# Cosine attention and a leaky-relu MLP in one kernel: a written instruction list up to the third batch's second unit, and float32 sums of the last three groups' exponentials on VectorE

## The chip, the cores and the metric

The kernel runs on one core of one Trainium2 chip. The metric is the device time of one execution in microseconds (us); three runs of the kernel before gave 415.45, 415.52 and 416.83, median 415.52.

## The reference

Inputs are q, k and v (8 batches, 12 heads, 448 positions, 64 per head), a scalar tau, and two weight matrices. What is computed, cut to what matters:

```python
q_n = q / (norm(q, axis=-1) + 1e-6);  k_n = k / (norm(k, axis=-1) + 1e-6)
scores = q_n @ k_n.T / tau            # tau = 0.1, per head
attn = exp(scores - max) / (sum(exp(scores - max)) + 1e-9)
x = (attn @ v) reshaped to (3584 tokens, 768)
h = x @ w_in                          # 768 x 2048
out = maximum(0.01 * h, h) @ w_out    # 2048 x 768, float32
```

## The kernel before

**Stages of attention.** Heads go in pairs; a slot is what is normalised at a time. Each slot's rows are loaded by a DMA that SP issues (`load_qk`, L141 to L163), squared on POOL (L218, L226; three slots at the start on ACT), summed on VectorE (L234, L240), turned into norms on ACT (`roots`, two small activations, L247 and L248) and scaled on VectorE (`normalise`, L255 to L272). For the first two batches TensorE transposes the result (L286) and VectorE copies it back (L327). From the third batch on, VectorE transposes it (L308) and six small DMAs of SP per unit spread it (L317). A unit is two pairs of heads; it has seven key tiles.

**Scores.** The score matmuls take 64 rows of the array (L348 for the first two batches, L419 after that) and write pairs of PSUM banks; ACT takes the exponential of 128x896 elements at a time into a bfloat16 tile `pe` (L357, L425). **Sums and products.** The row totals are matmuls with a weight of ones: for the first two batches `totals` (L368), then `group_products(g, None)` (L444): 7 key tiles x 4 strips x 2 halves, 56 matmuls of 64x32 weights and 448 columns. A logarithm and an exponential on ACT invert them (L379/L380, L453/L456). The products with v are 48 or 56 matmuls more per half of the head (L368, L444), and VectorE scales them into `xT` (L399, L469, L475). A group is one or two units (`GROUPS`): groups 7, 8 and 9, the last three, are units 12 to 17.

**The MLP.** Tokens go in eight chunks, 384 or 512 columns in turn. `first(c, m)` (L496) multiplies 6 slices of `w_in` with `xT` for each of 16 rows of blocks m; ACT applies the leaky relu into `hT` (L507), of which there is one buffer, so a chunk's relus wait for the chunk before to be read. `second(c, ts, half)` (L533) is 16 matmuls of 384 columns; VectorE copies the result (L543) and SP writes it out (L550).

**What sets the order.** Every engine runs its instructions in the order in which the program states them. The head of the program (the first two batches) is written as calls in loops and lists. From the third batch on, loops walk through *visits* of three key tiles; a planner with weights and due times feeds `first` and `second` groups between them. `fill` (L607) is a matmul on a constant tile that keeps TensorE running at the start; `WARM = 20` of them stand ahead of the first transposes. `hold` (L618) is a tiny POOL copy that makes POOL wait for a normalised slot before its next squares or DMA; `hold_loads` (L615) does the same on SP's queue. The eight PSUM banks are dealt by age, at the start with pairs and singles in separate halves.

Of the kernel before, what the change touches and what calls it, by code (L numbers as in the profile page):

```python
# [12 lines left out]
AX = mybir.AxisListType  # L13


@with_exitstack
def kernel(
# [25 lines left out]
    WARM = 20  # L43
    NEWQ = 2 * NQ
    PER = 3
# [5 lines left out]
    vbp = ctx.enter_context(tc.tile_pool(name="vb", bufs=3))  # L51
# [19 lines left out]
    age = [0] * 8  # L71
    kept = {}
    deals = {"n": 0, "apart": True, "width": 128}

    def banks(count, keep=None):
        lo, hi = (0, 8) if not deals["apart"] else (0, 4) if count == 2 else (4, 8)
        x = min(
            (i for i in range(lo, hi, count) if not set(range(i, i + count)) & set(kept.values())),
            key=lambda i: max(age[i : i + count]),
        )  # L80
        deals["n"] += 1
        age[x : x + count] = [deals["n"]] * count
        if keep:
            kept[keep] = x
        return ps[:, x] if count == 1 else ps[:, x : x + count]

    def given_back(keep):
        deals["n"] += 1
        age[kept.pop(keep)] = deals["n"]

# [21 lines left out]
    raw = {}  # L117
# [55 lines left out]
    def load_v(j):  # L173
        if j >= B * NQ:
            return
        b, jj = divmod(j, NQ)
        vb[j] = vbp.tile([128, 4, 3, D], BF16, name="v_b")
        gp.dma_start(out=vb[j], in_=main(v, b, 4 * jj, 4))
# [32 lines left out]
    def squares(s, eng=gp, parts=(0, 1)):  # L211
        if s >= NSLOT:
            return
        sq = sqt[s % 3]
        if s >= OLD:
            sqs[s] = sq
            x = raw[s].rearrange("p (t d) -> p t d", d=D)
            gp.tensor_tensor(sq[:, :, :D], x, x, op=ALU.mult)  # L218
            return
        sqs[s] = halves(sq.rearrange("p t d -> p (t d)"), D + 1)  # L220
        for i in parts:
            x, y = raw[s][i], sqs[s][i]
            if eng is nc.scalar:
                nc.scalar.activation(y[..., :D], x, func=AF.Square)
            else:
                eng.tensor_tensor(y[..., :D], x, x, op=ALU.mult)  # L226

    def sums(s, parts=(0, 1)):
        if s >= NSLOT:
            return  # L230
        if s not in ss:
            ss[s] = smp.tile([128, 14], F32, name="ss")
        if s >= OLD:
            nc.vector.tensor_reduce(  # L234
                ss[s], sqs[s], axis=AX.X, op=ALU.add
            )
            return
        for i in parts:
            o = ss[s][:, 0:8] if i == 0 else ss[s][:, 8:14]
            nc.vector.tensor_reduce(  # L240
                o.rearrange("p (h t) -> p h t", h=2), sqs[s][i], axis=AX.X, op=ALU.add
            )

    def roots(s):
        if s >= NSLOT:
            return
        nc.scalar.activation(ss[s], ss[s], func=AF.Ln)  # L247
        nc.scalar.activation(norms[s % 3][:, :, 0], ss[s], func=AF.Exp, scale=0.5)  # L248
# [3 lines left out]
    def normalise(s):  # L252
        if s >= NSLOT:
            return
# [29 lines left out]
    def one(tp, s, lo, hi):  # L284
# [10 lines left out]
    def transposed():  # L295
        return banks(1).bitcast(BF16)[:, : 7 * 128].rearrange("p (t c) -> p t c", c=128)
# [3 lines left out]
    def transposes(s):  # L300
        if s >= NSLOT:
            return
        if s >= OLD:
            u, which = divmod(s - OLD, 2)
            if which == 0:
                turned[u] = ttp.tile([128, 2, 2, S], BF16, name="tt")
            to = turned[u][:, :, which].bitcast(F32)
            nc.vector.transpose(  # L308
                out=to.rearrange(("p g (c m) -> p m g c", "p g (m c) -> p m g c")[which], m=7),
                in_=qn[s].bitcast(F32).rearrange("p m (g c) e -> p m g (c e)", g=2),  # L310
            )
            if which == 0:
                return
            for w, pair in enumerate(UNITS[u][1]):
                dst = qtp.tile([128, 2, S], BF16, name="qkT")
                for r0, of, n, g in ((0, 0, 32, 0), (32, 0, 64, 1), (96, 32, 32, 0)):
                    nc.sync.dma_start(  # L317
                        out=dst[r0 : r0 + n],
                        in_=turned[u][64 * w + of : 64 * w + of + n, g],
                    )  # L320
                qkT[pair] = dst.rearrange("p t c -> p (t c)")
            return
        dst = qtp.tile([128, 7, 128], BF16, name="qkT")
        qkT[s] = dst.rearrange("p t c -> p (t c)")
        tp = transposed()
        one(tp, s, 0, 7)
        nc.vector.tensor_copy(out=dst, in_=tp)  # L327
# [6 lines left out]
    def scores(s, kis):  # L334
        key_tiles([(s, ki) for ki in kis])

    def key_tiles(which):

        tiles = []
        for s, ki in which:  # L340
            sc = banks(2)
            tiles.append(sc)
            width = deals["width"] if ki < 3 else min(deals["width"], 64)
            for p in range(0, 128, width):
                x, c0 = (qkT[s - 1 + p // 64], 448 + p % 64) if ki == 3 else (qkT[s], 512 + 128 * ki + p)
                for a in range(2):
                    rows = slice(64 * a, 64 * a + 64)
                    nc.tensor.matmul(  # L348
                        out=sc[p : p + width, a, :S], lhsT=x[rows, c0 : c0 + width],
                        rhs=x[rows, 0:S], start=True, stop=True,  # L350
                    )
        for (s, ki), sc in zip(which, tiles):
            if ki == 3:
                dst = pr[s // 2] = pe_tile()
            else:
                dst = pe[s, ki] = pe_tile()
            nc.scalar.activation(out=dst, in_=sc[:, :, :S], func=AF.Exp, scale=inv_tau)  # L357
# [17 lines left out]
    def totals(j):  # L375
        sm = banks(1)
        strip_products(j, sm, lambda g, ki: ones, lambda g: ones_rem[:, g // 2])
        rb = rbp.tile([128, 2, S], F32, name="rb")[:, 0]
        nc.scalar.activation(rb, sm[:, :S], func=AF.Ln)  # L379
        nc.scalar.activation(rb, rb, func=AF.Exp, scale=-1.0)  # L380
        rbs[j] = rb

    pos = {}

    def products(j, e, po=None):
        b, jj = divmod(j, NQ)
        if po is None:
            po = banks(1, (j, e))
        pos[j, e] = po
        vm = vb[j].rearrange("p h t (d e) -> p h t e d", e=2)  # L390
        vr = vrb[b % 2].rearrange("p j g (d e) -> p j g e d", e=2)
        strip_products(j, po, lambda g, ki: vm[:, g, ki, e], lambda g: vr[:, jj, g, e])

    def scale(j, e):
        b, jj = divmod(j, NQ)
        m, half = divmod(b, 2)
        if m not in xT:
            xT[m] = xtp.tile([128, KT, 2 * S], BF16, name="xT")
        nc.vector.tensor_tensor(  # L399
            xT[m][:, 2 * jj + e, half * S : (half + 1) * S], pos.pop((j, e))[:, :S], rbs[j],  # L400
            op=ALU.mult,
        )
        if (j, e) in kept:
            given_back((j, e))
# [3 lines left out]
    def quad_tiles(which):  # L408

        tiles = []  # L410
        for u, i in which:
            sc = banks(2)
            tiles.append(sc)
            for strip in range(4):
                x = qkT[UNITS[u][1][strip // 2]]
                c0 = S + 64 * i + 32 * (strip % 2)
                for a in range(2):
                    rows = slice(64 * a, 64 * a + 64)
                    nc.tensor.matmul(  # L419
                        out=sc[32 * strip : 32 * strip + 32, a, :S], lhsT=x[rows, c0 : c0 + 32],  # L420
                        rhs=x[rows, 0:S], start=True, stop=True,
                    )
        for (u, i), sc in zip(which, tiles):
            pq[u, i] = pe_tile()
            nc.scalar.activation(out=pq[u, i], in_=sc[:, :, :S], func=AF.Exp, scale=inv_tau)  # L425
# [3 lines left out]
    def group_products(g, e):  # L429


        us = [u for u, (gg, _) in enumerate(UNITS) if gg == g]
        two = len(us) == 2
        po = banks(2)
# [14 lines left out]
        return po  # L449

    def group_logs(g, po):
        grb[g] = rbp.tile([128, 2, S], F32, name="rb")
        nc.scalar.activation(grb[g], po[:, :, :S], func=AF.Ln)  # L453
# [10 lines left out]
    def group_scale(g, e, po):  # L464
        js = GROUPS[g]
        for w in range(2):
# [6 lines left out]
            for n in range(2):  # L473
# [4 lines left out]
                )  # L478

# [7 lines left out]
    def first(c, m, kts=range(KT)):  # L487
        c0, n = chunk_cols(c)
        if c not in hT:
            hT[c] = htp.tile([128, MT, 512], BF16, name="hT")  # L490
        if (c, m) in begun:
            pm, done = begun.pop((c, m))
        else:
            pm, done = banks(1, (c, m, "begun") if len(kts) < KT else None), 0
# [7 lines left out]
        if done + len(kts) < KT:  # L502
            begun[c, m] = pm, done + len(kts)
            return
        if (c, m, "begun") in kept:
            given_back((c, m, "begun"))
# [491 lines left out]
```

## Time and profile before

| what | us |
|---|---|
| median of three runs | 415.52 |
| profiled execution, its own time | 416.8 |
| its span on the core | 415.0 |
| TensorE matmuls busy | 405.8 (98%) |
| ACT busy | 250.5 (60%) |
| VectorE busy | 221.4 (53%) |
| POOL busy | 115.1 (28%) |

The span runs from the first to the last instruction of the core; the execution's own time is 1.8 us longer. A line of the profile gives the source line, the engine, the operation with output and inputs, its count, the busy time and the mean duration of one. The chain of waits is the work that ended last, followed back; a row gives start, length and the line. TensorE's granted clock is 1.00 in all stretches.

### The profile page before, as it was taken

To read this page: it belongs to the slowest core of one execution; us is meant where nothing else is said; L and a number is where in the kernel's file an instruction comes from. 1 tells how busy PE (TensorE), PEld (TensorE's weight loads), DVE (VectorE), ACT (ScalarE), POOL (GpSimd) and SP (SyncE) were. 2 spreads that over 40 slices of the span, in tenths; PEclk is the share of its full clock that TensorE was granted. 3 is DMA by queue.
4 is the path that set the end of the run, shared out by engine and by line. 5 is a ranking of instruction groups with operands and counts; after the bars stand their busy time and mean duration, and the time that the engine had idled before them with its cause. 6 is when DMAs were issued, how large, how long until landed. Compare 5 with 4: busy or idle time off the path is not lost.

```text
span 415.0 us, 11326 instructions
## 1 busy us (share of the span) xinstructions
PE 405.8 (98%) x4783; PEld 212.2 (51%) x4799; DVE 221.4 (53%) x387; ACT 250.5 (60%) x431; POOL 115.1 (28%) x150
## 2 busy tenths in 40 slices
PE   8799999999999999999999999999999999999997
PEld 3235555544555555544455555554445555654465
DVE  5878879756778556766484964464621301210021
ACT  4997877378657785667865688547764464004300
POOL 4885556133234132413331433122210000000000
PEclk9999999999999999999999999999999999999999
DMA  7999998965377851884285681742442100020022
GB/s 184 233 208 222 216 232 176 258 178 127 57 208 184 206 127 24 206 230 97 51 190 153 149 235 44 173 128 84 91 90 66 53 39 3 38 77 0 2 76 76
DMA packets 41980, 53.82 MB, mean 130 GB/s; under 512 B 12490, under 2 KB 32330, under 8 KB 41930
## 3 DMA queue, kind: packets, MB, share of 16 engines
q1 hardware_dynamic: 25738, 41.01, 35.1%
q0 software_dynamic: 15504, 11.80, 19.8%
q8 instruction: 37, 0.61, 0.6%
q10 hardware_dynamic: 688, 0.30, 0.2%
q14 instruction: 13, 0.11, 0.1%
HBM read 45.61 MB, written 11.01 MB: 136 GB/s over the span
## 4 chain that ended last, share of the span: by engine, by line
PE 93%; DMA 2%; ACT 1%; POOL 1%; SPq 1%; issue 1%; DVE 0%; POOLq 0%
PE ps L533 36%; PE ps L496 36%; PE ps L444 9%; PE ps L419 7%; PE ps L368 3%; PE ps L348 2%; DMA xT<-in_k_dram 1%; DMA xT<-in_q_dram 1%; ACT pe L357 1%; POOL sq L226 1%; PE ps L286 1%; SPq L133 0%; DVE qn L272 0%; POOL v_rem L186 0%; SPq L141 0%
## 5 line engine op out<-in xcount | busy, mean ns | idle before, releaser
L533 PE MATMUL ps<-w_out_sb,hT 128*128 128x384 bf16 (+1 forms) x912 | 151.3, 323 | 0.0
L496 PE MATMUL ps<-xT,w_in_sb 128*128 128x384 bf16 (+1 forms) x754 | 150.1, 352 | 0.8 <-issue 0.2
L425 ACT ACTIVATE pe<-ps 128x896 bf16<-128x896 f32 x126 | 108.9, 916 | 47.1 <-PE ps L419 47.1
L533 PEld LDWEIGHTS <-hT 128*128 128x128 bf16 x912 | 86.5, 98 | 64.0 <-issue 10.3
L496 PEld LDWEIGHTS <-w_in_sb 128*128 128x128 bf16 x768 | 72.6, 98 | 74.3 <-issue 9.8
L507 ACT ACTIVATE hT<-ps 128x384 bf16<-128x384 f32 (+1 forms) x128 | 67.4, 553 | 56.1 <-PE ps L496 54.9
L543 DVE COPY osb<-ps 128x384 f32<-128x384 f32 (+1 forms) x57 | 31.2, 547 | 101.4 <-PE ps L533 101.3
L218 POOL TENSOR_TENSOR sq<-qk_h 128x896 f32<-128x896 f32 x36 | 60.9, 1691 | 13.0 <-DMA qk_h<-in_k_dram 8.5
L618 POOL CAST seen<-qn 128x1 f32<-128x1 bf16 x46 | 8.5, 185 | 166.3 <-DVE qn L262 156.5
L262 DVE TENSOR_TENSOR qn<-qk_h,r 128x896 bf16<-128x896 f32 x36 | 43.3, 1203 | 1.2
L234 DVE TENSOR_REDUCE ss<-sq 128x14 f32<-128x910 f32 x36 | 37.9, 1053 | 1.1 <-POOL sq L218 1.1
L357 ACT ACTIVATE pe<-ps 128x896 bf16<-128x896 f32 x42 | 36.0, 918 | 2.4 <-PE ps L348 2.3
L419 PE MATMUL ps<-qkT 64*32 64x448 bf16 x1008 | 36.5, 353 | 0.0
L255 DVE TENSOR_REDUCE r<-norms 128x14 f32<-128x28 f32 x48 | 8.6, 178 | 48.7 <-ACT norms L248 48.1
L469 DVE TENSOR_TENSOR xT<-ps,rb 128x448 bf16<-128x448 f32 x32 | 18.4, 615 | 23.2 <-PE ps L444 21.5
L308 DVE STREAM_TRANSPOSE tt<-qn 128x448 f32<-128x448 f32 x36 | 29.6, 821 | 0.9
L444 PE MATMUL ps<-pe,vq 64*32 64x448 bf16 x1008 | 27.0, 349 | 0.0
L247 ACT ACTIVATE ss<-ss 128x14 f32<-128x14 f32 x48 | 10.3, 215 | 23.6 <-DVE ss L234 23.1
L419 PEld LDWEIGHTS <-qkT 64*32 64x32 bf16 x1008 | 13.0, 91 | 19.2 <-issue 14.2
L444 PEld LDWEIGHTS <-vq 64*32 64x32 bf16 x1008 | 14.5, 92 | 8.0 <-issue 0.3
L444 PE MATMUL ps<-pe,ones 64*32 64x448 bf16 x560 | 15.1, 349 | 0.0
L348 PE MATMUL ps<-qkT 64*64 64x448 bf16 (+1 forms) x132 | 12.8, 359 | 2.1 <-ACT pe L357 1.2
(53 smaller groups left out, 218.1 us busy)
## 6 DMA issues: line engine op xcount, KB each, us to landing
qk_h<-in_q_dram SPq DMA_DIRECT2D x36, 224.0 KB, 4.1
qk_h<-in_k_dram SPq DMA_DIRECT2D x36, 224.0 KB, 4.6
out_dram<-osb SPq DMA_DIRECT2D x20, 384.0 KB, 2.3
qkT<-tt SPq DMA_DIRECT2D x72, 56.0 KB, 3.2
qkT<-tt SPq DMA_DIRECT2D x36, 112.0 KB, 3.4
vq<-in_v_dram POOLq DMA_DIRECT2D x16, 224.0 KB, 4.7
w_in_sb<-in_moe_w_in_dram POOLq DMA_DIRECT2D x4, 768.0 KB, 10.4
out_dram<-osb SPq DMA_DIRECT2D x15, 192.0 KB, 3.7
```

What stands on the lines that cost most here:

```text
L218: gp.tensor_tensor(sq[:, :, :D], x, x, op=ALU.mult)
L234: nc.vector.tensor_reduce(ss[s], sqs[s], axis=AX.X, op=ALU.add)
L262: nc.vector.tensor_tensor(qn[s].rearrange("p m d e -> p m e d"), raw[s].rearrange(f"p ({t[1:-1]} d) -> p m e d", e=n, d=D), r.rearrange(f" ...
L308: nc.vector.transpose(out=to.rearrange(("p g (c m) -> p m g c", "p g (m c) -> p m g c")[which], m=7), in_=qn[s].bitcast(F32).rearrange("p ...
L357: nc.scalar.activation(out=dst, in_=sc[:, :, :S], func=AF.Exp, scale=inv_tau)
L419: nc.tensor.matmul(out=sc[32 * strip : 32 * strip + 32, a, :S], lhsT=x[rows, c0 : c0 + 32], rhs=x[rows, 0:S], start=True, stop=True,)
L425: nc.scalar.activation(out=pq[u, i], in_=sc[:, :, :S], func=AF.Exp, scale=inv_tau)
L444: nc.tensor.matmul(out=po[32 * strip : 32 * strip + 32, w, :S], lhsT=weights, rhs=pq[us[x if two else 0], i][rows, a, :], start=(i == 0), ...
L496: nc.tensor.matmul(out=pm[:, :n], lhsT=w_in_sb[:, kt, m * 128 : (m + 1) * 128], rhs=xT[c // 2][:, kt, c0 : c0 + n], start=(done + i == 0), ...
L507: nc.scalar.activation(out=hT[c][:, m, :n], in_=pm[:, :n], func=AF.Prelu, alpha=0.01)
L533: nc.tensor.matmul(out=po2[:, : hi - lo], lhsT=hT[c][:, m, ts * 128 : (ts + 1) * 128], rhs=w_out_sb[:, m, half * HALF + lo : half * HALF + ...
L543: nc.vector.tensor_copy(out=o[:, cols], in_=po2[:, : hi - lo])
```

## The change

A string `ORDER` of 1,249 words now lists every step, and a loop calls them one after another; a word is a step's name with its numbers, as `f.0.5` for `first(0, 5)`. Steps that were one call are cut in two, so that the matmuls (`k`, `q`, `f`, `s`, `to`, `pr`, `g`) and what reads their banks (`x`, `y`, `r`, `o`, `ln`, `sc`, `gl`, `gx`) stand apart in the list. Three stretches can be told apart:

- **Up to `q.2.4`** (the fifth key tile of unit 2) the list is in a new order. 30 fills stand ahead of the first transposes instead of 20, and 9 after them instead of 19. PSUM is dealt as one pool from the start. `hold_loads` is gone, and most `hold`s.
- **From `q.2.4` up to `s.3.3.0.384`** TensorE's steps come as the visits had them.
- **From there on** the visits are replaced by a new order in which score tiles, `first` and `second` are mixed.

In the last stretch the row totals of groups 7, 8 and 9 are formed differently: VectorE adds the seven exponentials of a unit into a float32 tile (`a`, 6 additions of 128x896 for each of 6 units, 36 in all), and 8 float32 matmuls with ones take the place of 56 bfloat16 ones. Two float32 tiles serve all six units; they lie in the memory of the v tiles of the first two batches, and the float32 ones in that of the identity.

```diff
-    WARM = 20
-    PER = 3
+    whole = {}
+    def add_up(u, i, eng=nc.vector):
+        if i == 1:
+            whole[u] = sum_of[u % 2]
+        eng.tensor_tensor(whole[u], pq[u, 0] if i == 1 else whole[u], pq[u, i], op=ALU.add)
+    def ones_in_float():
+        nc.vector.memset(id128.bitcast(F32)[:, 0:32], 1.0)
-    def group_products(g, e):
+    def group_products(g, e=None):
+        if e is None and us[0] in whole:
+            ones_f = id128.bitcast(F32)[:, 0:32]
+            for strip in range(4):
+                for w in range(2):
+                    rows = slice(64 * w, 64 * w + 64)
+                    nc.tensor.matmul(
+                        out=po[32 * strip : 32 * strip + 32, w, :S], lhsT=ones_f[rows],
+                        rhs=whole[us[strip // 2]][rows, strip % 2, :], start=True, stop=True,
+                    )
+            return
+    for step in ORDER.split():
+        name, *args = step.split(".")
+        steps[name](*map(int, args))
```

The list at its start, up to the first full `first` group, and around the last three groups (cut):

```
sq.2.1 w.2 lq.6 w.20 w.2 w.2 qf.0.0.3 sq.2.0 qf.1.0.3 uf.0.0.3 qf.0.3.4 uf.1.0.3 uf.0.3.4 ro.0 no.0 sa.1.1
sa.1.0 su.1.0 tg lv.0 w.2 w.2 tp.0.0.4 tp.0.4.7 lr.0.0.2 ta.0.0.4 su.1.1 tc.0.4.7 sq.3.1 k.0.1 k.0.0 ro.1
su.2.1 sq.3.0 no.1 k.0.2 hr lr.0.2.4 tp.1 w.2 x.0.0 x.0.2 x.0.1 wi.0 sq.4.1 su.2.0 tc.1 k.1.3 k.1.2 lv.1 ro.2
...
f.0.3.0.1.2.3 f.0.2.0.1.2.3 ro.6 to.2 ro.7 ln.2 in.2 no.6 pr.2.1 pr.2.0 sc.2.1 tp.6 sc.2.0 f.0.5 f.0.3.4.5
...
lg.7 lg.8 sq.47 y.12.6 y.13.2 s.4.1.384.768 tt.43 o.4.2.384.768 a.13.1 a.12.4 a.13.2 o.4.1.384.768 f.5.11
f.5.2 f.5.7 f.5.9 f.5.0 sq.46 a.13.3 r.5.2 y.14.0 f.5.4 r.5.9 r.5.0 f.5.3 f.5.6 a.13.4 a.13.5 ro.45 r.5.4
ro.44 su.47 r.5.7 r.5.11 r.5.3 no.45 su.46 a.12.5 ro.46 td.15 a.13.6 a.12.6 r.5.6 q.14.4 q.14.1 q.14.3 y.14.4
f.5.14 f.5.5 no.46 no.44 q.14.5 y.14.1 y.14.3 r.5.5 ro.47 r.5.14 q.15.0 g.7 f.5.12 f.5.13 gl.7 f.5.10 f.5.1
tt.45 no.47 y.15.0 r.5.12 r.5.13 y.14.5 gi.7 q.15.1 q.14.6 g.7.0 y.15.1 a.14.1 y.14.6 tt.46 tt.47 a.15.1 tt.44
gx.7.0 f.5.15 f.5.8 q.15.3 q.15.4 r.5.10 r.5.1 r.5.15 g.7.1 y.15.3 r.5.8 q.15.2 y.15.4 s.5.1.0.384 gx.7.1
a.14.2 td.16 s.5.0.0.384 y.15.2 a.14.3 a.15.2 o.5.1.0.384 o.5.0.0.384 td.17 q.16.2 q.15.6 q.15.5 s.5.2.0.384
s.5.2.384.768 a.14.4 y.16.2 y.15.5 y.15.6 q.16.1 q.17.0 a.15.3 a.15.4 o.5.2.0.384 a.14.5 a.15.5 a.15.6
o.5.2.384.768 a.14.6 q.16.0 y.16.0 s.5.0.384.768 y.17.0 g.8 y.16.1 q.16.6 q.17.3 gl.8 y.16.6 y.17.3
...
r.6.6 r.6.14 r.6.8 g.9.1 g.9 r.6.1 s.6.2.0.384 gl.9 gi.9 s.6.0.0.384 gx.9.1 gx.9.0 f.7.15 s.6.1.0.384
```

## The prediction

> **What bounds the kernel now.** I read the busy table first, then the chain of waits, then TensorE's own waits, and then the timelines of the first 40 us and of the last third.
>
> ```profile
> PE 405.8 (98%) x4783; PEld 212.2 (51%) x4799; DVE 221.4 (53%) x387; ACT 250.5 (60%) x431; POOL 115.1 (28%) x150
> ```
>
> The chain, with start, length, line and count:
>
> ```profile
> 29.23 0.81 ACT pe L357
> ...
> 37.23 0.39 PE ps L286 x7
> 37.62 1.30 PE ps L496 x8
> ...
> 108.19 0.38 PE ps L419 x16
> 108.56 2.71 PE ps L533 x16
> 111.27 0.69 PE ps L419 x24
> 111.96 5.31 PE ps L533 x32
> 117.27 0.69 PE ps L419 x24
> ...
> 123.58 1.32 PE ps L444 x56
> ```
>
> The last ACT row stands at 29.23; from 30.1 on the chain is TensorE alone until 412.1, and TensorE's list of waits holds no more than 7 us, nearly all before 31. So after 31 us only less TensorE work, or a new wait, moves the end. The rows give its prices. 16 matmuls of 384 columns are 2.60 us (5.31 less 2.71), 0.163 each; 512 columns are 0.216. Matmuls on parts of the array run side by side: 56 in 1.32 us are seven rounds of eight, 0.188 a round. A change of the array's tiling costs 0.12: 24 score matmuls take 0.69, three rounds and 0.12 more; 16 that follow matmuls of the same tiling take 0.38, two rounds. These prices add up: from 37.62 to 117.27 TensorE has 75.7 us of matmuls and 33 changes of tiling, 79.7 together; the chain shows 79.65.
>
> The first 37 us are bound by ACT, not by TensorE: 25.40 us of ACT are busy between 10 and 40 us, mostly exponentials (0.83 us apart in a row). First come fills, whose weight loads show their pace:
>
> ```profile
> 6.75 0.15 PEld L607 LDWEIGHTS <-pe 128*128 128x128 bf16 x1 [0.28 <-issue]
> 7.17 0.15 PEld L607 LDWEIGHTS <-pe 128*128 128x128 bf16 x1 [0.28 <-issue]
> 7.54 0.96 PEld L607 LDWEIGHTS <-pe 128*128 128x128 bf16 x5 [0.21 <-issue]
> ```
>
> Until 7.5 us a fill takes 0.43, after that 0.21; the transposes that stand behind the 20 fills start at 8.83, though their input (`qn` of slot 0) was ready at 7.88.
>
> **The change, part by part.** *1. The head, up to `f.0.5`.* 30 fills instead of 20 stand ahead of the first transposes: ten more at 0.216 put these at 11.0, 2.2 us later, and the first exponential at 12.7 (before 10.37). What follows on ACT until the inverse of the third totals is the same work: 21 exponentials at 0.83 (17.4), six pairs of roots at 0.45 (2.7; before five came ahead of it), three pairs of logarithm and inverse at 1.1 (3.3): 23.4 us. Before, ACT needed 25.2 (10.37 to 35.52), with some 2 us of gaps, the longest of 0.64, 0.50 and 0.36, at places where an exponential waited for a score matmul or a copy of VectorE. In the new list scores run further ahead (one pool of banks), and I find VectorE's copies 1 to 1.5 us ahead of ACT from the third slot on; so I take no gaps, and the inverse ends at 36.5. VectorE then does two scalings (1.15 for both, behind the sixth `normalise`, which ends at 36.7): 37.9. `f.0.5` has four of its six slices done by then, 0.65 us that stood behind the corresponding point of before (37.46). So it is at 38.0 where before stood at 38.1: **-0.1 us**. If all of the 2.2 us remains, the head costs +2.1; if the fills cost nothing, it gains 1.5 more.
>
> DMAs of the head: without `hold_loads` the loads of slots 8 and 9 go out at about 17 and 20 us, not at 21.7 and 26.5, and compete with `w_in`. The four parts of `w_in` are issued at 16.5, 21.9, 25.3 and 27.1 (before 16.6, 20.1, 26.5 and 29.6, landing after 7.7 to 12.0 us). Even with 12 us the last is there at 39, and `f.0.10`, the first that needs it, comes at 43.5. The second half of `w_out` lands near 73 (issue 57.7 behind the squares of slot 12, 15.1 as before); its first use is at 75. Both are covered, the second by 2 us only. Most `hold`s go too; POOL, busy 28% of the span, has room for squares at any time, and a collision of them with `normalise` (below, 1 us) falls on VectorE, which is ahead.
>
> *2. From `f.0.5` to `q.2.4`.* The same matmuls in another order, 32 changes of tiling instead of 33: **-0.1**. Summed along the list, ACT and VectorE have 61 and 60 us of work beside 85 of TensorE, so neither is the bound.
>
> *3. From `q.2.4` to `s.3.3.0.384`.* TensorE's sequence is the same: 0.
>
> *4. The last stretch.* Three times 56 bfloat16 matmuls go: 3 x 1.32, less 3.96. Three times eight float32 ones come. No float32 matmul is in this trace. The nearest row is
>
> ```profile
> L444 PE MATMUL ps<-pe,ones 64*32 64x448 bf16 x560 | 15.1, 349 | 0.0
> ```
>
> One round of these is 0.19 us, the least for the eight; if float32 ones did not run side by side, eight at 0.35 would be 2.8, the most. Operands are twice as wide on both sides, so that a single round is unlikely; seven rounds, 1.32, is where the change would save nothing. I take the middle of 0.19 and 1.32, 0.75 a group: 3 x 0.57, **-1.7** (ends -3.4 and +4.4). The Trainium skill (FP8 and Floating Point Precision, section TensorE Precision Notes) says that true float32 takes four passes through the array. By that a group would cost four rounds, 0.75, and the sum would not change; no run here shows it yet.
>
> Changes of tiling in this stretch and the one before it, from `q.2.4` on: 71 instead of 75, **-0.5**.
>
> The 36 additions go to VectorE. Their nearest row is the scaling of 128x896 with two inputs in memory, and it comes in two sizes:
>
> ```profile
> 66.96 1.68 POOL L218 TENSOR_TENSOR sq<-qk_h 128x896 f32<-128x896 f32 x1 [1.46 <-DMA qk_h<-in_q_dram]
> 67.04 0.18 DVE L255 TENSOR_REDUCE r<-norms 128x14 f32<-128x28 f32 x1
> 67.26 0.24 DVE L256 RECIPROCAL r<-r 128x14 f32<-128x14 f32 x1
> 67.53 2.16 DVE L262 TENSOR_TENSOR qn<-qk_h,r 128x896 bf16<-128x896 f32 x1
> ```
>
> Alone it takes 1.17; here it lasts until 69.69, 1.05 after POOL's squares end at 68.64: it waited for them. The Trainium skill (SBUF — State Buffer, section SBUF: two separate sides) has it that a VectorE operation with two inputs in SBUF and a GpSimd one exclude each other for whole instructions. It speaks against the new additions, and this row agrees; but POOL has only the squares of slots 44 to 47 left beside them. I take 1.1 an addition, ends 1.05 and 2.16. VectorE was busy 42.5 of the 105 us from 240 to 345, so 40 more fit. Where the room is least: between `g.7` and `g.8` TensorE has 26.7 us (six groups of 512 columns at 1.30, five `s` at 2.60, two products at 1.31, 11 rounds of scores, some ten changes), VectorE 20.2 (12 additions, three transposes, four scalings at 0.58, four copies). From `s.4.1.384.768` to `g.7` TensorE has 17.0; VectorE needs 10.9 after the first 2.6, 3.5 to spare. Behind `g.8.0` it is 24.5 against 14.4. What is queued behind an addition are copies that free banks, scalings and normalisings; with these margins they are not late: 0.
>
> *Sum:* -0.1 - 0.1 - 1.7 - 0.5 = -2.4. The span of 415.0 becomes 412.6; the profiled execution's 416.8 becomes 414.4; the median 415.52 becomes **413.1**. The last matmuls and the final DMA (412.1 to 415.0) are unchanged.
>
> **The rivals.**
> *Head late (same):* ACT's gaps remain, and the ten fills cost their full 2.2 us. For it: `ta.0.0.4` and with it the whole chain of exponentials stand behind them. Against it: gaps ahead of exponentials depend on banks, which are freer. 415.52 - 2.3 + 2.1: 415.3.
> *Head early:* the fills are hidden, for example because TensorE's full pace comes sooner than 7.5 us. 411.6.
> *Float32 no cheaper:* eight float32 matmuls cost seven rounds: 414.8; if they run one after another, 419.2. For it: nothing in the trace shows float32 side by side. Against it: every other shape of this tiling runs so.
> *VectorE becomes the bound (slower):* an addition costs what the row of 2.16 shows. Then the 12 between `g.7` and `g.8` take 12.7 more, 6.2 over the margin; the six ahead of `g.7` 6.4 more, 2.9 over; the ten ahead of `g.9` 10.6 more, 0.5 over: 413.1 + 9.6 = 422.7. It decides from about 1.65 an addition on (3.5/6 and 6.5/12 above 1.1). Collisions with four squares alone, 4 x 1.68 ahead of `g.7`, would cost at most 3.2. Against it: POOL is idle after that.
> That the change doesn't do what it says is no rival: 4,655 matmuls instead of 4,799 are in the built program.
>
> **How the numbers follow.** Forecast 0.50, head early 0.08, head late 0.14, float32 no cheaper 0.12, VectorE the bound 0.16. About 0.5%, 2.1 us, is what a measurement of this kernel can tell from no change; faster means below 413.4, close to the forecast. Of the forecast's 0.50, 0.34 lie below that, 0.14 within, 0.02 above; float32 no cheaper is 0.08 within and 0.04 above. So faster 0.34 + 0.08 = 0.42, same 0.14 + 0.14 + 0.08 = 0.36, slower 0.02 + 0.04 + 0.16 = 0.22. The range leaves out the bound VectorE and the tail of float32: 410.8 (forecast with float32 at 0.3 a group and a head 1 us early) to 417.6 (waits of 3.2 us at `g.7` and some at the head).
>
> **What would show it.** Fills 0.43 apart until about 7.5 and transposes near 11.0; the first exponential near 12.7; ACT without gaps until 36.5; the first `f` group with six slices near 37.4; `q.2.4` near 117.0; float32 rounds of 0.75 a group; additions of 1.1 on VectorE; no wait of TensorE in the last third. A wait of TensorE for VectorE ahead of `g.7` or `g.8`, for `w_out` near 75, or a `q.2.4` later than 118 would make it wrong.

## The result and the profile after

The changed kernel takes **423.29 us** (median of six runs, 419.54 to 424.67); the kernel before takes 416.25 beside it (415.45 to 416.83). The ratio is 1.0155, with a 95% interval of 1.0129 to 1.0182: slower by about 7 us (1.3 to 1.8%), where 413.1 was predicted. The profiled execution took 423.35, its span 421.6. The runs scatter by 5 us, those of before by 1.4. A ratio leaves out runs more than 1.5% above the fastest of the same kernel; below that is one run, 427.53 of e13.

The busy table of the page and its row of TensorE's granted clock come first:

```profile
PE 406.6 (96%) x4663; PEld 212.5 (50%) x4679; DVE 270.3 (64%) x424; ACT 246.7 (59%) x431; POOL 113.3 (27%) x116
...
PEclk9879999999999999999999999999999999999999
```

TensorE's share has fallen, and in the second and third slice of 10.5 us its clock has an 8 and a 7, where before had nines throughout. Busy time has not fallen with the 144 fewer matmuls, since some of them ran at half pace (e4 below, with its clock at 1.00 throughout, has 404.2). The chain of waits (start, length, line, count) says where the time went:

```profile
12.53 2.78 DVE qn L358 x2
...
17.31 3.42 DVE qn L358 x2
...
124.31 0.69 PE ps L491 x24
...
397.50 20.86 PE ps L623 x144
```

The row at 124.31 is `q.2.4`; before it stood at 117.27. So **the head costs 7.04**. From there to the end of the last matmuls (418.36) it is 294.05, before 294.82 (117.27 to 412.09): **the rest gains 0.77**, not 2.2. The list of TensorE's waits from 8 us on (engine and line, whom it waited for, us in total, times, longest) names the new one:

```profile
PE ps L373 <- DVE qn L358: 6.9, 5, 1.9
PE ps L426 <- ACT qkT L389: 0.5, 1, 0.5
PE ps L587 <- DVE xT L563: 0.5, 1, 0.5
PE ps L587 <- issue: 0.5, 3, 0.2
PE ps L491 <- DVE osb L639: 0.3, 1, 0.3
...
```

The transposes (L373) wait for `normalise` (L358). Its timeline rows on VectorE, and those of POOL's squares (L305) and DMA issues in the same stretch:

```profile
12.51 2.79 DVE L358 TENSOR_TENSOR qn<-xT,r 128x512 bf16<-128x512 f32 x2
...
17.31 3.42 DVE L358 TENSOR_TENSOR qn<-xT,r 128x512 bf16<-128x512 f32 x2
...
22.35 1.16 DVE L358 TENSOR_TENSOR qn<-xT,r 128x512 bf16<-128x512 f32 x2
```

```profile
12.82 2.07 POOL L305 TENSOR_TENSOR sq<-xT 128x384 f32<-128x384 f32 x2
...
17.38 0.84 POOL L305 TENSOR_TENSOR sq<-xT 128x384 f32<-128x384 f32 x1
18.15 0.81 POOL L255 DMA_DIRECT2D shared<-in_v_dram  x1
18.98 3.42 POOL L305 TENSOR_TENSOR sq<-xT 128x512 f32<-128x512 f32 x3
```

A `normalise` of two parts takes 1.16 alone and 2.79 or 3.42 beside squares. Before, the `hold`s (L618) put the squares (L226) behind it, here for slot 1; only slot 2's met some (1.82):

```profile
10.72 1.16 DVE L272 TENSOR_TENSOR qn<-xT,r 128x512 bf16<-128x512 f32 x2
```

```profile
12.02 0.18 POOL L618 CAST seen<-qn 128x1 f32<-128x1 bf16 x1 [1.06 <-DVE qn L272]
13.11 2.27 POOL L226 TENSOR_TENSOR sq<-xT 128x512 f32<-128x512 f32 x2 [0.91 <-DMA xT<-in_k_dram]
```

In the changed kernel TensorE waits meanwhile. The table by stretches (length, then the busy time of PE, PEld, DVE, ACT and POOL, then the clock, the DMA share and GB/s) shows what follows:

```profile
10.00:16.00 6.00, 2.89 (x25) 1.43 (x24) 4.72 (x8) 3.51 (x7) 5.98 (x9) 1.00 1.02 234
16.00:18.00 2.00, 1.59 (x9) 0.33 (x8) 1.93 (x5) 1.46 (x4) 1.98 (x3) 0.74 1.34 269
18.00:20.00 2.00, 0.53 (x4) 0.35 (x4) 2.00 (x2) 1.45 (x2) 1.98 (x3) 0.50 1.23 233
20.00:22.00 2.00, 1.07 (x6) 0.34 (x6) 2.00 (x4) 0.60 (x3) 2.00 (x3) 0.50 1.11 197
22.00:24.00 2.00, 2.00 (x18) 0.62 (x22) 1.91 (x5) 2.00 (x3) 1.55 (x3) 0.50 1.06 195
```

After a stretch in which TensorE was busy for half of the time, its clock is 0.50, until 27. The row at 22.00 is full, and its matmuls take nearly twice their time (12 of L449 in 1.31 us, else 0.75). In two of the same stretches before:

```profile
18.00:20.00 2.00, 1.11 (x18) 0.34 (x10) 1.31 (x4) 1.97 (x4) 2.00 (x3) 1.00 1.03 139
20.00:22.00 2.00, 1.47 (x23) 0.73 (x23) 1.93 (x4) 1.78 (x4) 1.87 (x4) 1.00 1.07 183
```

A second loss stands at 57 us, where three squares catch `normalise` of slot 10 and TensorE waits 1.86 for it:

```profile
57.60 5.08 DVE L358 TENSOR_TENSOR qn<-qk_h,r 128x512 bf16<-128x512 f32 x2
```

### The profile page after: what moved, and what is told of

Read it like the earlier page. It is cut to its first block, busy times and chain, and to the rows that moved or that the text cites. A ratio compares the mean times of both kernels' runs of the same rounds, so it can differ in the third digit from the quotient of the medians.

```text
span 421.6 us, 11058 instructions
## 1 busy us (share of the span) xinstructions
PE 406.6 (96%) x4663; PEld 212.5 (50%) x4679; DVE 270.3 (64%) x424; ACT 246.7 (59%) x431; POOL 113.3 (27%) x116
## 4 chain that ended last, share of the span: by engine, by line
PE 84%; DVE 8%; DMA 4%; ACT 1%; SPq 1%; issue 1%; DVEq 0%
PE ps L623 32%; PE ps L587 31%; PE ps L537 8%; PE ps L491 7%; DVE qn L358 3%; PE ps L449 3%; DMA xT<-in_q_dram 2%; PE ps L426 2%; DMA qk_h<-in_q_dram 1%; DVE shared L507 1%; DMA qkT<-tt 1%; PE ps L373 1%; PE ps L523 1%; DVE qkT L389 1%; DVE ss L318 0%
## 5 line engine op out<-in xcount | busy, mean ns | idle before, releaser
L601 ACT ACTIVATE hT<-ps 128x384 bf16<-128x384 f32 (+1 forms) x128 | 64.8, 549 | 63.9 <-PE ps L587 45.8
L299 POOL TENSOR_TENSOR sq<-qk_h 128x896 f32<-128x896 f32 x36 | 63.1, 1758 | 88.8 <-DMA qk_h<-in_q_dram 39.0
L348 DVE TENSOR_TENSOR qn<-qk_h,r 128x896 bf16<-128x896 f32 x36 | 46.3, 1287 | 1.3
L491 PE MATMUL ps<-qkT 64*32 64x448 bf16 x1008 | 36.1, 352 | 0.3 <-DVE osb L639 0.3
L507 DVE TENSOR_TENSOR shared<-shared,pe 128x896 f32<-128x896 f32 x30 | 35.5, 1216 | 0.3
L703 POOL CAST seen<-qn 128x1 f32<-128x1 bf16 x12 | 2.4, 202 | 65.7 <-DVE qn L348 63.8
L281 POOL DMA_DIRECT2D vq<-in_v_dram x20 | 12.6, 639 | 25.6 <-PE ps L491 25.6
```

Of the source, the lines that this page charges most:

```text
L348: nc.vector.tensor_tensor(qn[s].rearrange("p m d e -> p m e d"), raw[s].rearrange(f"p ({t[1:-1]} d) -> p m e d", e=n, d=D), r.rearrange(f" ...
L491: nc.tensor.matmul(out=sc[32 * strip : 32 * strip + 32, a, :S], lhsT=x[rows, c0 : c0 + 32], rhs=x[rows, 0:S], start=True, stop=True,)
L507: eng.tensor_tensor(whole[u], pq[u, 0] if i == 1 else whole[u], pq[u, i], op=ALU.add)
L601: nc.scalar.activation(out=hT[c][:, m, :n], in_=pm[:, :n], func=AF.Prelu, alpha=0.01)
```

## The experiments

All kernels are the changed program with another `ORDER`; the list of before, written out in the same words, is called the old list. In a list `w.n` is n fills, `tp` transposes, `k` scores, `to` totals, `no.s` is `normalise` of slot s, `sq.s.p` a part of its squares, `su` their sums, `hp.s` a `hold` for it and `hs.s` a `hold_loads`. Below, "head" is the start of `q.2.4`, "rest" the time from there to the end of the last matmuls. Head and rest are read from the one profiled run of each kernel, and they scatter: the same old list has heads of 117.27, 116.75 and 117.22 (before, e1, e8), the same repaired list 116.54, 116.30 and 117.52 (e5, e12, e11). Differences of heads under about 1 us are no more than that scatter. Ratios are to the kernel before, whose median was 416.1 beside e1 to e15 and 416.25 beside the changed kernel.

| run | median us | ratio, 95% interval | head | rest |
|---|---|---|---|---|
| before | 416.1 | 1 | 117.27 | 294.82 |
| changed | 423.29 | 1.0155 [1.0129, 1.0182] | 124.31 | 294.05 |
| e1 old head, new rest | 415.44 | 0.999 [0.9979, 1.0] | 116.75 | 294.40 |
| e2 new head, old last stretch | 423.15 | 1.0167 [1.012, 1.0213] | 125.04 | 294.84 |
| e3 three holds | 418.19 | 1.0055 [1.0037, 1.0074] | 119.92 | 294.09 |
| e4 fills spread | 417.54 | 1.0045 [1.0022, 1.0068] | 119.08 | 293.07 |
| e5 fills and holds | 415.76 | 0.9988 [0.9978, 0.9998] | 116.54 | 293.60 |
| e6 old, 30 fills ahead | 418.61 | 1.006 [1.0045, 1.0075] | 119.11 | 294.84 |
| e7 old, no holds | 423.35 | 1.0168 [1.0151, 1.0185] | 122.51 | 294.84 |
| e8 old, float32 sums | 423.85 | 1.018 [1.0142, 1.0218] | 117.22 | 301.99 |
| e9 old, ten more fills | 417.47 | 1.0033 [1.002, 1.0045] | 118.71 | 294.84 |
| e10 changed, ten more fills | 420.55 | 1.0099 [1.0063, 1.0136] | 119.82 | 293.61 |
| e11 e5 without float32 | 417.59 | 1.0031 [1.0019, 1.0044] | 117.52 | 294.64 |
| e12 e5, additions later | 415.47 | 0.9985 [0.9971, 0.9998] | 116.30 | 293.60 |
| e13 changed, 22 more fills | 423.62 | 1.0111 [1.0072, 1.015] | 125.71 | 293.90 |
| e14 e7 with 14 more fills | 420.33 | 1.0104 [1.0087, 1.0121] | 120.50 | 294.84 |
| e15 e12, two more holds | 415.25 | 0.9977 [0.9964, 0.999] | 116.34 | 293.62 |

**Head or rest: e1 and e2.** e1 has the old list ahead of `q.2.4` and the changed list from it on; e2 has the changed list ahead of `s.3.2.384.768` and the old one from it on. At both places each engine has done the same set of steps in either list.

```diff
 e1
-sq.2.1 w.2 lq.6 w.20 w.2 w.2 qf.0.0.3 sq.2.0
+w.20 qf.0.0.3 uf.0.0.3 qf.1.0.3 uf.1.0.3
...
 q.2.4 y.2.4 q.2.5 q.2.6
 e2
 s.3.2.384.768
-su.38 o.3.2.384.768 fo ro.38 no.37
...
```

> The list of before up to q.2.4 (20 fills ahead, all holds), the changed list from q.2.4 on with the float32 sums. Theory: the loss lies in the head alone (q.2.4 at 124.31 instead of 117.27) and the tail gives 0.8 net, so 0.8 us faster than before, about 415.4, q.2.4 near 117.3. Rival 1, the tail waits only because the head shifts the loads against it: then 2.2 faster, about 414. Rival 2, the float32 sums or VectorE's additions cost elsewhere: no gain, or slower than before.

> The changed list up to s.3.2.384.768, then the visits of before with bfloat16 sums (no additions on VectorE). Theory: the whole loss of the head stays, 7.0 us slower than before, about 423.3, and the runs scatter by about 5 us as those of the changed kernel do. Rival (the tail loses too, by VectorE): about as before.

As expected: e1 stands 0.7 below before (its interval reaches 1.0), e2 loses the whole 7.0 and scatters (420.1 to 424.9). The float32 sums are not the cause of the loss.

**One of two: e3 and e4.**

e3 does at `no.1`, `no.2` and `no.10` what its first lines show; e4 puts three more groups of fills, 2, 3 and 2, ahead of `k.0.1`, `k.1.0` and `tp.2`.

```diff
 e3
-tc.0.4.7 sq.3.1 k.0.1
+tc.0.4.7 k.0.1
-sq.3.0 no.1
+no.1 hp.1 sq.3.1 sq.3.0
...
 e4
-lq.6 w.20 w.2
+lq.6 w.10 w.2
-k.0.2 hr
+k.0.2 w.3 hr
...
```

> The changed kernel with the squares of slots 3, 4, 11 and 13 put behind normalise of slots 1, 2 and 10, each with a hold ahead. Collision theory: the three normalise take 1.2 instead of 2.8 to 5.1, q.2.4 comes 4 to 5 us earlier than 124.3, the run takes about 418.5 to 419.5. Fill theory (ten more fills ahead and fewer between, TensorE's clock falls): the collisions go but the granted clock still falls between 16 and 28 us, 1 to 2 us earlier at most, about 422.

> The changed kernel with ten of the 30 fills ahead of the first transposes moved to four places between the first scores. Fill theory: first exponential near 10.4 instead of 12.3, the granted clock stays near 1.0 from 16 to 28 us, q.2.4 3 to 5 us earlier, about 419. Collision theory: first exponential 1.9 earlier, but VectorE is held by the squares as before, q.2.4 at most 2 us earlier, about 421.5, and the clock still falls where VectorE is late.

Each takes more than half of the loss, since in both the `normalise` of slot 10 takes 1.16 instead of 5.08. In e3, whose time is that of the collision theory, the three held `normalise` take 1.16, but the squares now meet that of slot 3, and the clock still falls:

```profile
14.84 1.16 DVE L353 TENSOR_TENSOR qn<-xT,r 128x512 bf16<-128x512 f32 x2
17.62 4.74 DVE L353 TENSOR_TENSOR qn<-xT,r 128x512 bf16<-128x512 f32 x2
```

```profile
18.00:20.00 2.00, 1.58 (x16) 0.47 (x15) 2.00 (x1) 2.00 (x3) 2.00 (x3) 0.51 1.25 224
20.00:22.00 2.00, 0.61 (x4) 0.34 (x4) 2.00 (x2) 0.76 (x2) 2.00 (x3) 0.50 1.08 193
```

In the profile of e4 the clock is 1.00 in every stretch, as the fill theory had it, though VectorE is held more often than in the changed kernel: five times in the first six slots (1.79 to 2.76) instead of twice. Its slot 10 squares miss `normalise` without a hold, so some 2.5 us of its gain (worked out below) are not the fills'.

**Both repairs: e5.** The repair of e4, and squares behind `normalise` of slots 1 to 5, 9 and 10.

```diff
-no.3 su.4.1 sq.5.0 tp.3 tc.3 sq.5.1
+no.3 hp.3 sq.5.0 sq.5.1 su.4.1 tp.3 tc.3
...
```

> The changed kernel with both repairs: ten of the 30 fills spread over four places, as in the run before (417.5, clock 1.00, q.2.4 at 119.08), and squares put behind normalise of slots 1 to 5, 9 and 10, each with a hold ahead. Collision theory: every normalise of two parts takes 1.16 and q.2.4 comes near 117.0, 414.5 to 415.5 in all. Rival (squares held back are late for their sums, so the delay only changes its place): q.2.4 near 119 still, about 417.

The head is back where it was: 116.54 in e5, within the scatter of the old list's 116.75 to 117.27. So the new order was not bad in itself. It needs none of the `hold_loads` on SP's queue, which e5 leaves out too. `normalise` takes 1.16, but for slots 3 and 6 (2.94 and 1.79).

**Each cause alone in the old list: e6, e7 and e9.**

e6 and e9 both have 30 fills ahead; e6 leaves out ten of the 19 behind them, e9 keeps all. e7 leaves out 21 holds.

```diff
 e6 and e9
-w.20 qf.0.0.3
+w.30 qf.0.0.3
 e7
-hp.0 sq.2.0 sq.2.1
+sq.2.0 sq.2.1
...
-hs.3 lq.8 hp.3 sq.5.0 sq.5.1
+lq.8 sq.5.0 sq.5.1
...
```

> The list of before with one thing changed: 30 fills ahead of the first transposes and 9 after them instead of 20 and 19; all holds stay, so no collisions. Clock theory in its strong form (fewer fills between are enough): the granted clock falls to 0.5 somewhere between 16 and 28 us and the run takes 419 or more. Weak form (the clock falls only where collisions leave TensorE idle as well): clock 1.00, only the first exponential later by 1.5 to 2, q.2.4 near 118.5, 417 to 418. Rival (the later start is caught up, ACT has gaps): about 416.

> The list of before with one thing changed: the holds on POOL and SP that the changed list lacks are left out up to q.2.4; the fills stay at 20 and 19. Collision theory: normalise of several early slots takes 2 to 5 us instead of 1.16, the clock stays near 1.00 thanks to the fills between, q.2.4 1.5 to 2.5 later, 417.5 to 418.5. Rival (VectorE has the slack that the prediction counted on): about 416.

> The list of before with 30 fills instead of 20 ahead of the first transposes and all 19 others left where they were, so 49 in all: the later start alone. With the ten taken from between, the run took 418.6, q.2.4 came at 119.11 instead of 117.27 and the granted clock was 0.5 from 16.5 to 19.9 us. Start theory: the clock stays 1.00 and q.2.4 still comes 1.5 to 2 later (ACT does not catch up), 417.5 to 418. Clock theory: most of that loss was the clock, so q.2.4 within 0.5 of before, about 416.3.

The fills ahead delay the head by 1.44 at full clock (e9) and by 1.84 when ten are missing between (e6); by the medians it is 1.4 and 2.5, and e9's profiled run (418.22) was one of its longest. In e6 the clock is half for 3.4 us although no wait of TensorE was over 1.3:

```profile
14.00:16.50 2.50, 0.57 (x6) 0.22 (x6) 2.43 (x7) 1.81 (x5) 2.50 (x4) 1.00 1.18 281
16.50:20.00 3.50, 3.17 (x17) 1.39 (x19) 2.44 (x5) 2.62 (x5) 3.50 (x6) 0.51 1.04 169
```

The missing holds alone cost 5.24 of head in the profiled run, the shortest of four (422.33), and 7.2 us by the median (e7), more than twice what I expected: the `normalise` of slot 3 takes 3.44 and the clock falls here too, with all fills in place.

```profile
18.00:22.00 4.00, 1.14 (x18) 0.37 (x6) 3.69 (x5) 2.95 (x5) 3.99 (x6) 1.00 0.99 153
22.00:26.00 4.00, 3.17 (x31) 0.93 (x35) 3.93 (x9) 1.08 (x3) 3.65 (x5) 0.63 1.20 225
```

**The clock alone: e10, e13, e14.** Fills are added where TensorE waits, and the collisions stay. e10 and e13 are the changed list, with 30 fills ahead; the places are those of e4, with 2, 3, 3 and 2 fills in e10 and 4, 8, 6 and 4 in e13. e14 is e7's list with 4 and 10.

```diff
 e10
-k.0.2 hr
+k.0.2 w.3 hr
...
 e14
-x.2.1 to.0
+x.2.1 w.4 to.0
-x.2.2 tp.3
+x.2.2 w.10 tp.3
```

> The changed kernel with ten more fills at four places between the first scores; the 30 ahead and all collisions stay. Clock theory: the granted clock stays 1.00 through the collisions, q.2.4 comes near 120.5 instead of 124.31, 419.5 in all, and the difference to the run with ten spread (119.08, 417.5) is the later start, about 1.5. Rival (the delay is VectorE's, the clock only follows): q.2.4 at 123 or later, 422 or more.

> The changed kernel with 22 more fills at four places between the first scores (4, 8, 6, 4); the 30 ahead and all collisions stay. Clock theory: the granted clock stays 1.00 in all runs, the scatter falls from 6 us to 1.5, about 418.5 (the 417.5 of the run with ten spread, and 1.0 for the later start, less or more by the fills themselves). Rival (scatter and loss are VectorE's collisions): 421 or more, and the scatter stays.

> The list of before without the holds (423.35, q.2.4 at 122.51, clock 0.5 from 23 to 26 us) with 14 more fills where TensorE waited, ahead of the totals and the transposes of slot 3. Clock theory: clock 1.00, q.2.4 near 120.5, 419.5 to 421: of its 7.2 the clock is 2 or more. Rival (there the collisions are nearly all): 422.5 or more.

In e14 the clock holds (0.999 to 1.0 in four runs) and the collisions stay, but for that of slot 11 (2.64 in e7, 1.16 here). The row of slot 3 is e7's, and half a us later than e7's half clock began it is still 1.00:

```profile
19.20 3.44 DVE L351 TENSOR_TENSOR qn<-xT,r 128x512 bf16<-128x512 f32 x2
```

```profile
23.50:24.00 0.50, 0.50 (x14) 0.12 (x4) 0.50 (x2) 0.10 (x1) 0.50 (x2) 1.00 1.28 216
```

By the medians 3.0 of e7's 7.2 went with the clock and 4.2 stayed with the collisions; by the heads of the two profiles it is 2.0 of 5.2. The clock theory had that.

In e10 the ten fills did not keep the clock: it is 0.57 from 14 to 18 us in the profile. The profiled run gained 4.5 of head all the same, and the six runs lay between 417.6 and 423.8. In e13 the clock held through the first 60 us of the profile, yet four runs lay between 419.1 and 427.5. That fits neither theory as I put it. The traces show a third thing, **a race at slot 10**. In e10 `normalise` starts 0.85 ahead of the squares and is done in 1.16; the POOL row says that the squares waited for it:

```profile
55.39 1.16 DVE L353 TENSOR_TENSOR qn<-qk_h,r 128x512 bf16<-128x512 f32 x2
```

```profile
56.24 1.85 POOL L294 TENSOR_TENSOR sq<-qk_h 128x896 f32<-128x896 f32 x1 [0.40 <-DVE qn L353]
```

In the changed kernel the squares start 0.27 ahead (57.33 against 57.60) and it takes 5.08. In e13 it took 6.46, TensorE waited 3.24, and the clock fell again:

```profile
60.00:62.00 2.00, 0.00 (x0) 0.00 (x0) 2.00 (x1) 0.00 (x0) 2.00 (x3) 1.00 1.31 204
62.00:64.00 2.00, 1.55 (x15) 0.94 (x19) 1.34 (x3) 0.00 (x0) 1.48 (x2) 0.56 0.90 116
```

A fraction of a us decides over 2.5 us or more. The kernels with a hold there scatter little (e3 1.6, e5 1.5, e11 1.9, e12 2.6, e15 2.2; before up to 2.6), those of the new head without it more (changed 5.1, e2 4.8, e10 6.2, e13 8.4; of e4's ten runs one took 421.7 and nine at most 418.2). The clock is not needed for it: two runs of e13 with mean clocks of 1.000 and 0.999 took 419.12 and 422.64. That the longer times are lost races is inferred; only profiled runs show one.

**The float32 sums: e8, e11, e12.**

e8 adds the 36 additions to the old list, one behind each transpose, scaling, copy or second relu; e11 takes them out of e5's list, so that the ones are bfloat16 again; e12 moves two of e5's.

```diff
 e8
-f.4.7 r.4.7 f.4.8
+f.4.7 r.4.7 a.12.1 f.4.8
...
 e11
-lq.46 a.12.2 y.13.5
+lq.46 y.13.5
...
 e12
-lq.46 a.12.2 y.13.5
+lq.46 y.13.5
-su.45 a.12.3 tt.42 o.4.1.0.384 o.4.2.0.384
+su.45 tt.42 o.4.1.0.384 o.4.2.0.384 a.12.2 a.12.3
```

> The list of before with the float32 sums alone: 36 additions on VectorE put into the visits of the last three groups, 24 float32 matmuls for 168 bfloat16 ones. Theory: 3 x 0.57 less on TensorE and no wait: 1.7 faster than before, about 414.4. Rival: additions hold up copies that free banks or the group products, which gives back 1 us or more: 415.5 or slower.

> The repaired changed kernel (fills spread, holds put back: 415.76) with the bfloat16 sums again: no additions on VectorE, 168 matmuls in the place of 24 float32 ones. Theory: 3 x 0.57 more on TensorE, less the 0.6 of waits that the additions cause near 275 and 290: 1.0 to 1.7 slower, 416.8 to 417.4. Rival (the additions cost as much as they save): 415.8 or less.

> The repaired changed kernel with two additions (a.12.2 and a.12.3) put behind one transpose and two copies that free banks. Theory: the wait of 0.35 for such a copy at 275 goes, 0.3 to 0.6 faster than 415.76, about 415.3. Rival (VectorE is full from 264 to 298, so the delay comes up again at the next group product): no change.

In the new list they are worth 1.04 of the rest (e11 against e5) and some 1.8 of the medians, of which 0.4 lies outside the span (e11's runs take 2.1 to 2.2 us more than their spans, e5's 1.7 to 1.8); where the remaining 0.4 comes from is open. In the old list they lose 7.2: VectorE is full from 266 to 289, and the float32 ones (L519) wait for an addition.

```profile
PE ps L519 <- DVE shared L503: 4.0, 2, 3.4
```

```profile
276.00:280.00 4.00, 3.25 (x30) 1.36 (x28) 4.00 (x4) 0.26 (x2) 1.72 (x2) 1.00 0.32 72
280.00:284.00 4.00, 1.34 (x16) 0.36 (x20) 3.93 (x7) 0.98 (x2) 0.00 (x0) 0.74 0.74 192
284.00:288.00 4.00, 3.78 (x18) 1.21 (x12) 3.86 (x5) 3.53 (x5) 1.82 (x2) 0.50 0.16 65
```

One wait of 3.4 and then half the clock to about 289: the wait is paid twice. In e12 the wait of 0.35 for a bank is gone, yet the rest is the same 293.60, with another wait of 0.5 (of `first`, L582, for `xT`, near 238). Its median, 415.47, is not told apart from e5's 415.76.

**The last two collisions: e15.**

```diff
-no.2 hp.2 sq.4.1 sq.4.0
+no.2 hp.2 sq.4.1
-no.3 hp.3 sq.5.0 sq.5.1
+no.3 hp.3 sq.4.0 sq.5.0 sq.5.1
...
-no.6 pr.2.1
+no.6 hp.6 sq.9.1 sq.9.0 pr.2.1
```

> The repaired changed kernel with the later additions (415.47) and the squares of slots 4 and 9 put behind normalise of slots 3 and 6 too, the last two that take more than 1.16 (2.95 and 1.79). Collision theory: 0.5 to 1.5 faster, about 414.5. Rival (squares now late for their sums, or ACT is the bound there): 415.5.

All `normalise` of the head take 1.16, and the head is as long as in e12 (116.34, 116.30), as the rival had it. TensorE's waits for `normalise` fall from 1.3 to 0.4, but those for a DMA of `w_in` grow from 0.5 to 0.8. The prediction had that DMA covered, which the delayed kernels did not put to the test. At 415.25 this is the lowest median here, 0.2% below before (at least 0.1% by its interval) and not told apart from e12's 415.47.

## Why the prediction was wrong

**The head, -0.1: the failed step.** It measured +7.04. Transposes at 10.62 and the first exponential at 12.27 came as worked out (11.0 and 12.7). What failed is "a collision of them with normalise (below, 1 us) falls on VectorE, which is ahead". VectorE was ahead in the old schedule because the holds kept squares off it; without them the old list loses 5.24 of head (e7). I had the row of a collision and the sentence on exclusion in the text, and used them on the additions alone. Split by single profiles, against e5: the lost race at slot 10 is 2.5 (at slot 9 the changed kernel stands 5.2 behind e5, 49.88 against 44.65, at `q.2.4` 7.8), the collisions up to there 2.5 (e4 less e5, clock 1.00 in both), the later start with the half clock 2.7 (changed less e4 at slot 9, 49.88 against 47.19). With e5's own -0.73 that is the 7.0. These are steps between kernels, good to about 1 us each, and not parts of one trace: the changed kernel's two `normalise` held before slot 9 took 3.9 us more than 1.16 each, e4's five 6.0. How the 2.7 divides stays open: e9 gives 1.44 for the start in the old list; e10 less e4 gives 0.74, with a half-clock stretch in e10 and none in e4.

**"ACT without gaps".** Wrong for the same reason: ACT was busy 3.51 of 6.00 us from 10 to 16 and 0.60 of 2.00 from 20 to 22, and the inverse of the third totals ended at 41.47 instead of 36.5. (Its terms add up to 36.1; the 0.4 changes nothing, since the scalings were put behind a `normalise` ending at 36.7.) The ten fills were not absorbed even without collisions (e9: 1.44 of the 2.2). That was the rival "head late" (+2.1), whose size was about right and whose place in the sum was too small.

**The clock, no term at all.** I noted that it was 1.00 everywhere and did not ask what kept it there: the fills between the first scores, ten of which were moved. e14 shows that fills inside the waits can keep the clock (e10's ten did not). No rival had it. By the Trainium skill (TensorE: Matmul & The Clock Gate, section HAM oscillation — how this bites in real kernels) a gap of more than some 3.4 us brings the clock down; here it fell with no wait over 1.9 (changed) or 1.3 (e6), so for this kernel the rule is too mild. The same page (the Trainium skill, TensorE: Matmul & The Clock Gate, section What's actually happening) puts the decision on a free-running window of 3413 ns; the half-clock stretches of 3.41, 6.83 and 10.24 us (last section) agree with that.

**From `q.2.4` to the last stretch, 0.** Right: e2's rest is 294.84, before's 294.82.

**Float32, -1.7.** The price of a group was right. The changed kernel's chain has the three rounds:

```profile
300.85 0.75 PE ps L523 x16
...
328.13 0.91 PE ps L523 x16
...
360.32 0.75 PE ps L523 x16
```

0.75 each, with 0.16 more where the tiling changes; the four passes of the Trainium skill (FP8 and Floating Point Precision, section TensorE Precision Notes) agree with that. What was left of the 1.7 in the rest was 1.04 (e5 against e11). An addition took 1.22 on average instead of 1.1:

```profile
L507 DVE TENSOR_TENSOR shared<-shared,pe 128x896 f32<-128x896 f32 x30 | 35.5, 1216 | 0.3
```

**Changes of tiling, -0.5 and "no wait".** In e4, where nothing waits after `q.2.4`, the rest gained 1.75 of the 2.2; without float32 (e11) the new order is worth 0.2, not 0.5. Waits take the other part: 1.1 after `q.2.4` in the changed kernel (`xT` 0.5, `osb` 0.3, issue 0.3). The rival "VectorE becomes the bound" is not what happened in this list, though e8 shows how near it is: with the same additions placed by the old visits it cost 7.2.

## What to carry to other kernels

Before a wait is taken away, ask what it kept apart: here the holds kept two engines off each other, and an engine that "is ahead" in a trace may be so only because of them. A stall of TensorE is priced twice when its clock can fall, once for the wait and once for the matmuls at half pace behind it, so fills belong where it waits. A run-to-run scatter that appears with a change can point to a race, as here between POOL's squares and a `normalise` that TensorE waits for.

## What the runs showed of the hardware

- The clock fell without a long gap: after 2.5 us at 0.57 busy (e6), 4 us at 1.14 (e7). In the 3.41 us ahead of the first fall TensorE was busy for 0.4 us in e13, 0.6 in e7, 1.3 in e6, 1.6 in the changed kernel and 1.9 in e3; in the kernels whose profiles show 1.00 throughout, no 3.41 us between 9 and 70 had less than 1.8 (e4). So the busy share seems to decide, near 1.8 to 1.9 of 3.41 us in these profiles. Read at half a us, with a mean between 0.5 and 1 taken as a mixture of the two, the half-clock stretches were 3.41 us long in e6, e7 and e10, 6.83 in e3 and 10.24 in the changed kernel: one, two and three times 3.41.
- POOL operations in a row can keep a waiting VectorE operation out: 5.08 us for work of 1.16 behind three squares at slot 10. They do not always: the `normalise` that the changed kernel starts at 17.31 is done at 20.73, while the row of three squares from 18.98 runs to 22.40. In e13 it was not let in during the 0.96 us of a DMA issue between squares either (6.46), while in e8 an addition ended 0.94 after a square, beside such an issue (297.59 to 299.11). What decides this is open.
- Eight float32 matmuls on parts of the array are recorded as 16 and take 0.75, four rounds of 0.188.
